# Last two pairs of f tiles in another order on TensorE, last stores in other pieces, and a new order of all work

## The chip, the cores and the metric

The kernel runs on one core of one Trainium2 chip. The metric is the device time of one execution in microseconds (us). The kernel before has a median of 643.3 us over 3 runs, 641.54 to 643.62 us. The engines are PE (TensorE, matrix products; PEld is its loading of weights), DVE (VectorE), ACT (ScalarE), POOL (GpSimd) and SP (SyncE, which here only issues transfers). "SPq" and "ACTq" in rows are the sequencers that issue a transfer (DMA).

## The reference

There are 8 batches with 8 heads, 576 tokens and head size 64. Each batch first attends from 32 packed queries `p` to all keys and values, then from all tokens to those 32 packed results; the outcome goes through a feed-forward network with an ELU.

```
p_packed = softmax(p k^T / sqrt(64)) v          # per batch and head: 32 x 64
x        = softmax(q p_packed^T / sqrt(64)) p_packed
x        = x as 4608 tokens x 512
h        = x @ w_in                              # 512 -> 2048
g        = where(h > 0, h, exp(min(h, 0)) - 1)
out      = g @ w_out                             # 2048 -> 512
```

All inputs and outputs are float32.

## The kernel before, in words

**Stages.** Per batch, the packed attention (scores at L637, exponentials L654, transposition L783, product with `v` L815, transposition of the packed result L851, `ppT`), then the scores of the tokens against the 32 packed results (L876) and their softmax on DVE and ACT (L887 to L929). The product x @ w_in is folded: the packed result times `w_in` is made once per batch (L998, `m_hi`/`m_lo`), and the hidden layer is a product of the attention weights `a` with it. The hidden layer has 16 tiles of 128 rows ("f tiles"). Precision comes from splitting each float32 operand into a high and a low part in a rounded format, so that three products stand for one.

**Stretches.** The tokens of a batch are worked in two windows of 256 and 320 tokens. 512 of the 576 tokens go through the windows; the 64 left over of each batch are stored in DRAM (`rest_dram`) as hidden rows, and those of four batches together are worked off as one more stretch of 256 tokens beside the windows of the last batch. In the first two batches each f tile is a product with `w_out` of its own (L1543, then L1658 to L1661). From batch 2 on, two f tiles are worked as a pair by a scheme with seven products of halves in place of eight (`strassen_pair`).

**One pair.** L1271 makes the hidden rows in PSUM (12 matmuls). ACT and DVE make the ELU (L1283, L1286, L1278) in a buffer `w8`; for the left-over stretch the rows are loaded from `rest_dram` into a buffer `kvq` instead (L1290). Three sums of blocks follow (L1353, on DVE or POOL), then the split into high and low part: a cast on ACT (L428) and a subtraction on DVE (L1361), both into a buffer `g`, of which there are three. The product, L1426, has four groups, one for each of four accumulators in PSUM: 6, 6, 6 and 3 matmuls. The third factor of the groups comes from `swa` (three buffers) and `swb` (two), which SP loads from DRAM for every pair (L1386), and from `wo_a`/`wo_b`, which stay in SBUF.

**The end of a stretch.** After its last pair, a copy on ACT and five additions on DVE (L1458: `add1` and `add2`, `add3`, `add4`, `add5`) make two rows of 128 x 512 outputs out of the four accumulators. `add1` needs the first, `add2` and `add3` the second, `add4` the third and `add5` the fourth. The left-over stretch (in `kvq`) and the last batch's window (in `part`) have their own first three accumulators; the fourth is one PSUM bank for both, so `add5` of the left-over stretch waits until the window's last product in it is done (`run["rest5"]`, L1496). Stores are at L1500: two rows of 256 KB for the left-over stretch, and for the window three pieces: half a row (128 KB), a row on ACT's queue (256 KB), half a row (128 KB).

**The order.** Nothing is scheduled at run time. A table, `ORDER`, lists all 3327 operations in the sequence in which they are written out; the letter behind a number is the engine, where there is a choice. Each engine works its instructions in that sequence and waits on semaphores. `PLACES` gives the PSUM banks. `ONES` says after which operations how many filler matmuls on a tile of ones are issued (L435, `warm_up`), which keep PE busy in the start, where it has no data yet. Operations marked `two` make POOL wait for DVE's last such instruction.

Of the kernel before, what the change touches and what calls it, by code (L numbers as in the profile page):

```python
# [25 lines left out]
0 2 1 7 8 9 10 11 403 404V 405 406V 14 12 416 417V 17 15A 16A 3 4 20 18A 19A 21 13 23A 22A 24 25A  # L26
418 408 5 26 409V 410 400 401A 27 28 29 6 37 48 424 30 425A 402 411 31 32 33 34 529 530A 747 38 39
407G 55 35A 426 412A 413 754 531 748 755 749 40 49 50 56 532A 750 756 751A 414V 757 415G 752G 57 761
41 59 42 758A 759G 43 36 44 419 420A 58 421 753 62 762 763 432 60 65 422V 760 433A 63A 64A 764 768
440 441A 434 442 533 765A 766V 51 61 66A 67V 45 423G 769 534 535 52 770 771 68 69A 435 436A 772V  # L30
773V 775 782 70A 71 437 776 783 767 438V 777 778 72A 551 784 793 427 428A 552 456 439V 785 779A 780G
457A 786A 53 429 430A 431G 557 553 73 794 795 558 458 801 74 75 554 443 444A 787V 796 76 445 802 803
774 797 448 449A 781 450 798V 799G 451 559 77 804 446A 555 447G 806 807A 808G 78 556 810 811 812 813
814 560 561 46A 818 819 820 79 459 788 800 562 80 821 47 54 95 102 789A 805 81 815A 816G 823 84 791A
85 822 452A 453 536 537 824A 827 828 460A 825G 86 87 454A 835 836 837 461 829 455G 840 831 809 830
491 96 817 826 838 538 88 89 832A 833G 82A 83 462A 841A 844 845 90 842V 91 92 504 846 97 852 848 847
463G 505A 499 506 834 843 103 93A 853 94 865 854 492A 849V 850G 855 857 104 858A 106 872 851 866 867
# [12 lines left out]
1013 573 1011 1038A 1045A 115 117A 656G 657G 574 116V 1039V 1046V 658V 540 665V 666G 1031 1048 1049  # L50
1055 1027 1040 1056 1057 1058 1050 655 100 101 142 1051 1032 1062 1069 1052A 663V 664G 659A 660V
1059V 1005 1028 1053V 1063 1060G 1064 1047 1054 1070 1065 661V 662V 667 1066A 1067G 1061 1071 1072
1076 1083 1073A 1074G 1068 1029 1077 1084 1030 669V 1078 541 548 1085 670G 1086 654 1079 549 671V
1080V 1087A 542 543 550 1033 544 1081G 676A 678A 679G 681 677V 672V 118 119A 1088V 1075 673G 1096
1097 1104 120 143 1098 1100 674A 1099 675G 1090 131 1101A 1102G 1113 1082 1105 668 1114 1106 1115
121 122 123 124 125 1109 1089 1103 1110A 144 682G 1107 1116 1117 683V 1118A 1108 1119V 1111V 1121
1122 1123 1124 1130 1126 1127A 684V 689V 1128V 691V 1112 1120 1131 1132 1133 1134 685A 686V 1138
1091 687A 1125 1139 1140 1143 1141 1129 1135A 1136V 1144V 1093 1094 1095 1145G 1147 1155 126 690G
1148 1137 1146 1149 1156 1151 1157 1160 1150 1158 1092 1152A 1153V 127 128 1170 132 133 1161A 1159
1142 688G 1162G 692G 1171 1172 1173 1178 1179 1180 1181 680 1174 1175A 1154 1163 1183 1167 1184A  # L60
1187 1195 695V 1176V 1188 1189 1164 1177 134 1185V 1191 1190 1196 1186 1192A 696G 1182 1168 1169
1193G 1165 1166 1224 697V 698V 135 704V 1197 1200 1194 705G 707 1198 1199 1201A 1204 1212 1202V 1203
1205 1206 699V 700V 701V 1208 1207 1213 1214 1217 1215 1209A 1210V 1218A 1219G 1227 1234 1211 136
137 1228 1229 1230 1241 1235 1236 1237 1220 149 1231A 1232V 1233 138 139 1238A 694 1239G 1242 1243
1244 1225 1248 1245A 1246V 693 702V 703V 708V 709V 1249 706 1250 1251 1255 1256 710V 1257 1258 1252A
1253G 1221 1222 1223 1240 1247 715A 716V 1259A 1260V 717A 711A 712V 713A 714V 719 1262 1269 718V
1283 575 578 1263 1264 1265 721V 722G 720 1270 1271 1226 1272 576 577 1266A 1267V 1276 723V 129A
730A 1254 1261 130 731V 733 728A 729V 724A 725V 726A 727V 581 732 1273A 1274V 734V 579 1289 1286
1268 1275 1277 1278 1279 735G 580 736V 140A 1280A 1281V 737V 1298 738G 1313 582 583 1290 1304 743A
744V 739A 740V 1291 741A 742G 150 152 1292 746 153 154 745 156 157 1305 151 1282 1319 155 1287 584  # L70
1306 1307 1293G 1294G 1284 1295G 1296 1297 1334 1320 141 158 1308V 1309V 1310G 1321 1322 1323V 1324V
1325V 1311 1312 1299 159 162 1326 1327 1335 1336 1337 1338G 145 1339G 1328 1300 1301 1302 1303 1340G
160 1314 164 1349 1315 1316 1343 1350 1317 1318 1351 1352 1353G 1354G 585 1330 1331 586 1355V 1332
1341 1342 1356 1364 1288 1365 1357 1366 1329 1333 1367 1368V 1369V 1370G 1379 1380 1381 1382 1383V
1345 163 1346 1344 1347 1348 1360 1358 1361 165 146 1384V 1385V 1371 1372 1386 1387 1394 1395 166
167 1416 1396 161 1417 1418 1397 1420 1398G 1419 1362 1399V 168 169A 1359 1363 1375 1400V 1421 1373
1388 1401 170V 171 172A 1216 1402 1422 1423 1424 1426 1438 1439 1440 1441 1427G 1428V 1376 1377 1443
1374 1378 1442 1444 1445 1448 1446 147 148 173 1429G 1430 1449G 1450G 174 175 176 1285 1425 1431
# [116 lines left out]
    "623476764764674507501234454664670460126723064647676765045614653204545465456450456120457365777777"  # L195
    "7777032105674333330"
)
ONES = {0: 3, 8: 8, 17: 4, 21: 3, 24: 2, 26: 16, 529: 7}


@with_exitstack
def packed_attention_elu_ffn(
# [22 lines left out]
    nc = tc.nc  # L225
# [3 lines left out]
    NF = w_in.shape[0]  # L229
# [1586 lines left out]
```

## Time and profile before

| | |
|---|---|
| median of 3 runs | 643.3 us (641.54 to 643.62) |
| the profiled execution's own time | 642.62 us |
| its span, first to last instruction | 640.8 us |
| PE, PEld, DVE, ACT, POOL busy | 98%, 88%, 83%, 65%, 26% |
| granted PE clock over the span | 0.998 |
| moved by DMA | 160.43 MB, 250 GB/s on the mean |

In the timeline a row has the start in us from the span's first instruction, the duration in us, the engine, the source line, the operation, the output tile, `<-` and the input tiles, the sizes, and `xN` where N instructions are merged into one row. In square brackets stands how long the engine had been idle before and what ended the wait. A matmul's row is longer than its slot, because matmuls overlap: the distance between the starts of two rows tells the rate, not the length.

### The profile page before, as it was taken

The numbers are of one execution on the slowest core, as the hardware profiler recorded it, in microseconds if no ns is written. First come the engines' busy times: TensorE is split into PE (matmuls) and PEld (weight loads), VectorE is DVE, ScalarE is ACT, GpSimd is POOL, SyncE is SP. The second block draws the span as 40 slices with busy tenths as digits, with TensorE's granted clock in tenths as the row PEclk, the third lists the DMA queues.
The fourth block names the chain that finished last, engine by engine and source line by source line (L and its number), as shares of the span: only waits on it lengthen the run. The fifth ranks groups of instructions, "written<-read, shape, count | busy, mean of one in ns | idle before, by whom it ended". The sixth has DMA issues, their size and how long they took to land.

```text
span 640.8 us, 16120 instructions
## 1 busy us (share of the span) xinstructions
PE 630.3 (98%) x6130; PEld 561.9 (88%) x6130; DVE 534.7 (83%) x1093; ACT 418.9 (65%) x796; POOL 164.9 (26%) x258
## 2 busy tenths in 40 slices
PE   9999999999999999999999999999999999999996
PEld 4567988889789888999989897999889998999996
DVE  3999988779999789878886998898788989667756
ACT  3789987566677657755776577656566667545452
POOL 1224223433232311222123232123111322113121
PEclk9999999999999999999999999999999999999999
DMA  9985795656489978887888989888877777565762
GB/s 346 374 279 197 246 320 166 230 158 225 143 296 307 277 240 280 286 299 231 297 277 276 269 264 317 271 296 301 252 267 272 224 217 245 170 201 189 230 195 82
DMA packets 85405, 160.43 MB, mean 250 GB/s; under 512 B 24272, under 2 KB 40144, under 8 KB 85200
## 3 DMA queue, kind: packets, MB, share of 16 engines
q1 hardware_dynamic: 85040, 158.88, 75.3%
q8 instruction: 48, 0.79, 0.5%
q10 hardware_dynamic: 288, 0.52, 0.2%
q14 instruction: 29, 0.24, 0.1%
HBM read 132.90 MB, written 26.48 MB: 249 GB/s over the span
## 4 chain that ended last, share of the span: by engine, by line
PE 85%; DVE 5%; DMA 5%; ACT 1%; issue 1%; POOL 1%; SPq 0%; DVEq 0%; POOLq 0%; ACTq 0%
PE psum L1426 37%; PE psum L1271 20%; PE psum L1543 6%; PE psum L998 4%; PE psum L1658 4%; PE psum L1661 4%; PE psum L1659 4%; PE psum L435 2%; PE psum L815 2%; DMA kvq<-in_qT 2%; DMA swb<-swb_dram 2%; PE psum L876 1%; DMA out<-part 1%; PE psum L1536 1%; DVE part L1458 1%
## 5 line engine op out<-in xcount | busy, mean ns | idle before, releaser
L1353 POOL TENSOR_TENSOR w<-w 128x128 f32<-128x128 f32 (+1 forms) x167 | 93.8, 565 | 298.5 <-DVE w L1278 77.7
L428 ACT CAST g<-w 128x896 fp32r<-128x896 f32 x96 | 90.0, 940 | 61.2 <-POOL w L1353 28.7
L1361 DVE TENSOR_TENSOR g<-w,g 128x896 fp32r<-128x896 f32 x96 | 104.6, 1092 | 16.6 <-ACT g L428 15.6
L1271 PE MATMUL psum<-a_hi,m_hi 128*128 128x256 f32 (+1 forms) x384 | 112.5, 293 | 0.0
L1271 PE MATMUL psum<-a_lo,m_hi 128*128 128x256 f32 (+1 forms) x384 | 110.2, 287 | 0.0
L1271 PE MATMUL psum<-a_hi,m_lo 128*128 128x256 f32 (+1 forms) x384 | 110.2, 287 | 0.0
L1426 PE MATMUL psum<-wo_b,g 128*128 128x256 f32 x672 | 94.2, 276 | 0.0
L1426 PE MATMUL psum<-wo_a,g 128*128 128x256 f32 x672 | 93.8, 276 | 0.0
L1426 PE MATMUL psum<-swa,g 128*128 128x256 f32 x672 | 93.5, 275 | 0.2 <-DMA swa<-swa_dram 0.2
L1426 PEld LDWEIGHTS psum<-wo_b,g 128*128 128x128 f32 x672 | 84.3, 192 | 4.8 <-issue 4.0
L1426 PEld LDWEIGHTS psum<-wo_a,g 128*128 128x128 f32 x672 | 84.3, 192 | 3.1 <-issue 1.3
L1426 PEld LDWEIGHTS psum<-swa,g 128*128 128x128 f32 x672 | 84.4, 192 | 0.4 <-DMA swa<-swa_dram 0.4
L1271 PEld LDWEIGHTS psum<-a_hi,m_hi 128*128 128x128 f32 x384 | 73.2, 191 | 9.5 <-issue 2.8
L1271 PEld LDWEIGHTS psum<-a_lo,m_hi 128*128 128x128 f32 x384 | 73.3, 191 | 0.1
L1271 PEld LDWEIGHTS psum<-a_hi,m_lo 128*128 128x128 f32 x384 | 73.2, 190 | 0.0
L1283 ACT ACTIVATE e<-psum 128x320 f32<-128x320 f32 x96 | 41.2, 431 | 31.9 <-PE psum L1271 31.3
L1426 PE MATMUL psum<-swb,g 128*128 128x256 f32 x336 | 56.5, 277 | 0.8 <-DMA swb<-swb_dram 0.6
L1426 PEld LDWEIGHTS psum<-swb,g 128*128 128x128 f32 x336 | 46.6, 192 | 3.4 <-issue 2.2
L1278 DVE SCALAR_TENSOR_TENSOR w<-e,psum 128x256 f32<-128x256 f32 x96 | 39.1, 414 | 9.8 <-ACT e L1286 8.4
L1286 ACT ACTIVATE e<-e 128x320 f32<-128x320 f32 x96 | 44.4, 470 | 2.5
L1353 DVE TENSOR_TENSOR w<-w 128x128 f32<-128x128 f32 (+1 forms) x121 | 40.8, 342 | 6.0 <-POOL w L1353 3.8
L1278 DVE SCALAR_TENSOR_TENSOR w<-w,psum 128x512 f32<-128x512 f32 x48 | 32.7, 683 | 13.7 <-ACT w L1286 12.2
(143 smaller groups left out, 1222.5 us busy)
## 6 DMA issues: line engine op xcount, KB each, us to landing
swa<-swa_dram SPq DMA_DIRECT2D x96, 512.0 KB, 5.0
swb<-swb_dram SPq DMA_DIRECT2D x96, 256.0 KB, 4.0
kvq<-in_v SPq DMA_DIRECT2D x16, 640.0 KB, 6.2
raw<-in_w_out SPq DMA_DIRECT2D x16, 511.8 KB, 5.5
raw<-in_w_in SPq DMA_DIRECT2D x16, 511.8 KB, 6.1
kvq<-in_kT SPq DMA_DIRECT2D x14, 576.0 KB, 6.2
kvq<-in_qT SPq DMA_DIRECT2D x14, 576.0 KB, 5.7
out<-part SPq DMA_DIRECT2D x28, 256.0 KB, 4.5
```

The costliest lines, as they stand in the source:

```text
L428: (nc.scalar.copy if e == "ACT" else nc.vector.tensor_copy)(out=out, in_=in_)
L998: nc.tensor.matmul(ps.t[cols_of(pair), g, :w], lhsT=st.ppT.t[rows_of(g), pair, :], rhs=w_in_sb[rows_of(g), pair, c * FC + part * w:c * FC ...
L1271: nc.tensor.matmul(ps, lhsT=m_b[p].t[:, g, o:o + P], rhs=in_turn(st.a.t[q][:, g, cols]), start=(n == 0), stop=(n == 3 * G - 1),)
L1278: nc.vector.scalar_tensor_tensor(out=out, in0=e_, scalar=-1.0, in1=ps, op0=ALU.add, op1=ALU.max)
L1283: nc.scalar.activation(out=out, in_=ps, func=AF.Relu, scale=-1.0)
L1286: nc.scalar.activation(out=x, in_=x, func=AF.Exp, scale=-1.0)
L1353: eng(e).tensor_tensor(out=out, in0=x, in1=y, op=o)
L1361: nc.vector.tensor_tensor(out=g_b.all[:, 7 * P:(7 + b1 - b0) * P], in0=blocks(b0, b1), in1=g_b.all[:, :(b1 - b0) * P].bitcast(F32), op=ALU ...
L1426: nc.tensor.matmul(a.t[:, at * H:(at + rhs.shape[1]) * H], lhsT=operand(blk, p), rhs=rhs, start=new and n == k == 0, stop=a.final == (u, m ...
L1543: nc.tensor.matmul(ps_b.t[:, :n_tok], lhsT=m_b[x].t[:, g, o:o + P], rhs=in_turn(st.a.t[y][:, g, cols]), start=(n == 0), stop=(n == 3 * G - 1),
L1658: nc.tensor.matmul(a.t, lhsT=g_b.t[0][:, t], rhs=w[0], start=first, stop=False)
L1659: nc.tensor.matmul(a.t, lhsT=g_b.t[0][:, t], rhs=w[1], start=False, stop=False)
```

## The change

Four parts. (1) In the last two pairs of the last batch, the pairs are written out together: both pairs of the left-over stretch first, then both pairs of the last window; and the window's groups are chained by accumulator: the fourth accumulator of both pairs, then the first, the second and the third. (2) At the end of a stretch that is the second window of the last batch, `add5` comes before `add4`, the first row is stored in one piece after `add5`, and the second row in two halves after `add4`, one on SP's queue and one on ACT's. (3) `ORDER`, `PLACES` and `ONES` are new throughout. (4) An option that was off (`MIX`) is gone, and the buffers that a pair shares are kept per pair (`shared[u]`).

```diff
-0 2 1 7 8 9 10 11 403 404V 405 406V 14 12 416 417V 17 15A 16A 3 4 20 18A 19A 21 13 23A 22A 24 25A
...
+0 2 1 7 8 9 10 11 ... (all of the table is new)
-ONES = {0: 3, 8: 8, 17: 4, 21: 3, 24: 2, 26: 16, 529: 7}
+ONES = {0: 3, 8: 10, 17: 2, 21: 8, 24: 2, 529: 8, 37: 11}
...
-    MIX = 0
+    N_TAIL = 2
...
             a.last = run["out"]
-            if both and MIX:
-
-                a.last.after = [run["pair"].pop(0)]
-                for x in run["pair"][:1]:
-                    x.after = [a.last]
-            else:
-                run["pair"].append(a.last)
+            if both and win and u >= NF // 2 - N_TAIL:
+                tail.append(a.last)
...
+            late = both and win
+            if late:
+                y = op(q, {"DVE": 0.42}, add5, [y, acc[3].last], use=[part, acc[3]])
+                y5 = y
             y = op(q, {"DVE": 0.69}, add4, [y, acc[2].last], use=[part, acc[2]])
             y4 = y
-            y = op(q, {"DVE": 0.42}, add5, [y, acc[3].last], use=[part, acc[3]])
+            if not late:
+                y = op(q, {"DVE": 0.42}, add5, [y, acc[3].last], use=[part, acc[3]])
...
-            if both:
+            if late:
+                op(q, {"DMA": 0.7}, lambda e: store(e, (0,)), [y5], use=[part])
+                op(q, {"DMA": 0.5}, lambda e: store(e, (1,), slice(0, H)), [y], use=[part])
+                op(q, {"ACT": 0.1}, lambda e: store(e, (1,), slice(H, E), nc.scalar), [y], use=[part], lag=2.7)
+            elif both:
                 op(q, {"DMA": 0.5}, lambda e: store(e, (0,), slice(H, E)), [y3], use=[part])
...
             if f % 2 == 0:
+                late = b == B - 1 and win and f >= NF - 2 * N_TAIL
                 if b == B - 1:
                     strassen_pair(i, B + win, 0, f)
-                strassen_pair(i, b, win, f)
+                if late and f < NF - 2:
+                    continue
+                for n in reversed(range(N_TAIL if late else 1)):
+                    strassen_pair(i - 2 * n, b, win, f - 2 * n)
...
+    before = tail[0].after
+    for x in [tail[n + 4 * m] for n in (3, 0, 1, 2) for m in range(N_TAIL)]:
+        x.after, before = before, [x]
```

**PE's last matmuls before.** Four pairs of 21 matmuls follow each other: left-over and window of the last pair but one (`g_8911`, `g_8929`), then left-over and window of the last pair (`g_8938`, `g_8978`). Of the four, the rows of the last three:

```order
L1426 MATMUL psum_102<-wo_b_969,g_8929 128x256 x6
L1426 MATMUL psum_102<-swa_8780,g_8929 128x256 x6
L1426 MATMUL psum_102<-wo_b_969,g_8929 128x256 x6
L1426 MATMUL psum_102<-swb_8946,g_8929 128x256 x3
L1426 MATMUL psum_102<-wo_b_969,g_8938 128x256 x6
L1426 MATMUL psum_102<-swa_8973,g_8938 128x256 x6
L1426 MATMUL psum_102<-wo_b_969,g_8938 128x256 x6
L1426 MATMUL psum_102<-swb_8976,g_8938 128x256 x3
L1426 MATMUL psum_102<-wo_b_969,g_8978 128x256 x6
L1426 MATMUL psum_102<-swa_8973,g_8978 128x256 x6
L1426 MATMUL psum_102<-wo_b_969,g_8978 128x256 x6
L1426 MATMUL psum_102<-swb_8976,g_8978 128x256 x3
```

PE's last matmuls now; `g_8943` is the left-over stretch's last pair (its last but one, `g_8861`, stands just ahead), `g_8946` and `g_8960` are the window's last two pairs:

```order
L1424 MATMUL psum_102<-wo_b_1015,g_8943 128x256 x6
L1424 MATMUL psum_102<-swa_8963,g_8943 128x256 x6
L1424 MATMUL psum_102<-wo_b_1015,g_8943 128x256 x6
L1424 MATMUL psum_102<-swb_8975,g_8943 128x256 x3
L1424 MATMUL psum_102<-swb_8917,g_8946 128x256 x3
L1424 MATMUL psum_102<-swb_8975,g_8960 128x256 x3
L1424 MATMUL psum_102<-wo_b_1015,g_8946 128x256 x6
L1424 MATMUL psum_102<-wo_b_1015,g_8960 128x256 x6
L1424 MATMUL psum_102<-swa_8922,g_8946 128x256 x6
L1424 MATMUL psum_102<-swa_8963,g_8960 128x256 x6
L1424 MATMUL psum_102<-wo_b_1015,g_8946 128x256 x6
L1424 MATMUL psum_102<-wo_b_1015,g_8960 128x256 x6
```

The number of matmuls is the same. The fourth accumulator (the rows with `swb`) is done 36 matmuls before the end, and the window's last `g` is needed 18 matmuls earlier than before.

**DVE's last additions before** (`kvq` is the left-over stretch, `part` the window; 128x2x256 is `add2`, 128x512 is `add4`):

```order
L1458 TENSOR_TENSOR kvq_8987<-kvq_8987,psum_102 128x512
L1458 TENSOR_TENSOR part_85<-part_85,psum_102 128x256
L1458 TENSOR_TENSOR part_85<-part_85,psum_102 128x2x256
L1458 TENSOR_TENSOR part_85<-part_85,psum_102 128x256
L1458 TENSOR_TENSOR kvq_8987<-kvq_8987,psum_102 128x256
L1458 TENSOR_TENSOR part_85<-part_85,psum_102 128x512
L1458 TENSOR_TENSOR part_85<-part_85,psum_102 128x256
```

DVE's last additions now:

```order
L1451 TENSOR_TENSOR kvq_8971<-kvq_8971,psum_102 128x512
L1451 TENSOR_TENSOR kvq_8971<-kvq_8971,psum_102 128x256
L1451 TENSOR_TENSOR part_85<-part_85,psum_102 128x256
L1451 TENSOR_TENSOR part_85<-part_85,psum_102 128x2x256
L1451 TENSOR_TENSOR part_85<-part_85,psum_102 128x256 x2
L1451 TENSOR_TENSOR part_85<-part_85,psum_102 128x512
```

The left-over stretch is finished before the window begins, and the window's `add4` is the last instruction.

**ACT in the start before**, from its first exponentials (L654) on; `tops` is the first of two steps that turn a loaded weight tile (`raw`) into words, `ppT` the packed result of batch 0:

```order
L654 ACTIVATE tmp,sm<-psum,mx 128x576 x2
L428 COPY tmp<-psum 128x512
L428 COPY tmp<-psum 64x128
L428 COPY tmp<-psum 128x512
L428 COPY tmp<-psum 64x128
L837 ACTIVATE pp<-psum,ri 128x64 x2
L428 COPY ppT<-psum 128x128
```

ACT in the start now:

```order
L428 CAST tops<-raw 128x512 x2
L654 ACTIVATE tmp,sm<-psum,mx 128x576 x2
L428 COPY tmp<-psum 128x512
L428 COPY tmp<-psum 64x128
L428 COPY tmp<-psum 128x512
L428 COPY tmp<-psum 64x128
L428 COPY ppT<-psum 128x128
```

Two casts of weights, of the first tile of `w_out` and of `w_in`, which DVE did before, stand ahead of the exponentials, and the scaling L837 has gone to DVE. On SP the third tile of `w_in` is loaded ahead of the first part of `q`, and not behind it. On PE, by `ONES`, 8 fillers stand between L815 and L851 and not 3; between the first and the second L876 stand the first L998 and 8 fillers, and not 16 fillers; and the first two f tiles' hidden products (L1536, now L1542) are followed by two more, and not by one, before the first product with `w_out`. In batch 1's exponentials, two `tops` casts and a cast of `g` stand between the two L654 on ACT, where before there were an L1561 and an L1567.

## Rows read from the trace of the kernel before

**Rows 1.** The profile's page: the span, and PE's share of it.

```profile
span 640.8 us, 16120 instructions
PE 630.3 (98%) x6130; PEld 561.9 (88%) x6130; DVE 534.7 (83%) x1093; ACT 418.9 (65%) x796; POOL 164.9 (26%) x258
```

**Rows 2.** PE's waits: line, what ended it, us in total, times, longest.

```profile
PE psum L1658 <- ACT tmp L654: 1.5, 1, 1.5
...
PE psum L876 <- DMA kvq<-in_qT: 0.8, 2, 0.5
PE psum L1426 <- DMA swb<-swb_dram: 0.6, 1, 0.6
```

**Rows 3.** Timeline of the start, all engines.

```profile
9.02 0.74 ACT L654 ACTIVATE tmp<-psum,mx 128x576 f32<-128x576 f32 x1 [6.81 <-DVE mx L648]
...
12.19 1.73 PE L815 MATMUL psum<-kvq,tmp 128*32 128x64 f32 x80
...
14.58 0.33 PE L851 MATMUL psum<-ident,pp 128*128 128x128 f32 x1
...
15.27 0.66 PE L876 MATMUL psum<-q,ppT 64*32 64x256 f32 x16
15.87 3.63 PE L435 MATMUL psum<-part 128*128 128x512 bf16 x16
...
16.20 0.77 ACT L428 CAST tops<-raw 128x512 f16<-128x512 bf16 x1 [0.98 <-DMA raw<-in_w_in]
...
20.91 0.71 DVE L929 STREAM_TRANSPOSE k<-tmp 128x512 f32<-128x512 f32 x1
...
22.08 1.89 PE L1536 MATMUL psum<-k,m_hi 128*128 128x256 f32 x8
```

**Rows 4.** Timeline of PE alone, two products of batch 1's attention.

```profile
33.59 1.50 PE L815 MATMUL psum<-kvq,tmp 128*32 128x64 f32 x80
...
40.81 0.72 PE L876 MATMUL psum<-kvq,ppT 64*32 64x288 f32 x16 [0.21 <-DMA kvq<-in_qT]
```

**Rows 5.** Loads of `w_in` issued at 2.10 and 5.97: KB, us to landing.

```profile
raw<-in_w_in SPq DMA_DIRECT2D x1, 511.8 KB, 6.9
...
raw<-in_w_in SPq DMA_DIRECT2D x1, 511.8 KB, 10.1
```

**Rows 6.** The chain that ended last, pieces near 380: start, us, what.

```profile
380.55 1.63 SPq L1225
382.23 4.28 DMA swa<-swa_dram
```

**Rows 7.** Timeline of the end, all engines.

```profile
625.87 0.95 ACT L428 CAST g<-kvq 128x896 fp32r<-128x896 f32 x1 [0.26 <-PE psum L1426]
...
627.39 1.62 DVE L1361 TENSOR_TENSOR g<-kvq,g 128x896 fp32r<-128x896 f32 x1
...
630.62 1.09 DVE L1361 TENSOR_TENSOR g<-w,g 128x896 fp32r<-128x896 f32 x1 [1.61 <-ACT g L428]
...
631.63 2.27 DVE L1458 TENSOR_TENSOR kvq<-kvq,psum 128x256 f32<-128x256 f32 x4
...
632.70 0.83 PE L1426 MATMUL psum<-wo_b,g 128*128 128x256 f32 x6
...
633.98 1.65 DVE L1458 TENSOR_TENSOR part<-part,psum 128x256 f32<-128x256 f32 x3
...
634.71 0.50 PE L1426 MATMUL psum<-swb,g 128*128 128x256 f32 x3
635.55 0.41 DVE L1458 TENSOR_TENSOR kvq<-kvq,psum 128x256 f32<-128x256 f32 x1
...
635.88 1.01 DVE L1458 TENSOR_TENSOR part<-part,psum 128x512 f32<-128x512 f32 x2
```

**Rows 8.** Stores to `out` issued at 635.66 and at 637.05: KB, us to landing.

```profile
out<-part SPq DMA_DIRECT2D x1, 128.0 KB, 1.8
...
out<-part SPq DMA_DIRECT2D x1, 128.0 KB, 2.8
```

More of the change, by code (lines that the diff above doesn't have):

```diff
@@ new lines @@
+1447 173 1463 1466 1467 1468 1469 1390 1391 1392 1464 1393 1405 174 1470 1471G 1433 175 176 1452
+1482 1453 1487 1483 1484 1485 1486 1488 1406 1472G 1409A 1410 1473V 1489 1490 1492 1493G 1411 1412
+1407 1408 1413 1494G 1495V 1414 1474 1475 177 1432 1454 1476 1504 1509 178 1505 1506 1510 1511 1434
+1435 1436 1437 1456 1457 1458 1508 196 1514 179 1496 1507 1512 1526 1527 1531 184 180 181 1455 1477
+1459 1497 1515V 1516V 1491 1528 1529 1530 1415 1478 1532 1533 1534 1536 1548 185 1553 1517G 1518
+1479 1480 182A 186 187 1513 1481 183 1519 1537V 1538G 1549 188 1498 1550 1552 189 1500 1501 1554
@@ new lines @@
+1594 1646 1647 1590 1591 1595 1617 1616 1665 1649 1650 1651 213 1652 1653 1596 209 1638 596 1597 212
+215 1636 1666 1667 1668 1659 1654V 1618 1670 1655G 1656G 216 1681 217 1671 1672 1669 218 1619 1620
+1675 1673 1639 1676V 1677V 1678G 1674 1687 1692 597 1640 1657 1641 1658 1688 1693 1689 1690 1642
+1691 1661 1694 1695 1660 1679 1697 1709 1714 1710 1698G 1699G 598 1680 1696 1700G 1711 1712 1713
+1715 1716 1719 219 220 1662 1663 1664 1717 1701 1702 1731 1736 1732 1733 1737 1738 1720V 1721G 1722V
@@ new lines @@
+1913V 1925 1882 1926 1927 1897 1914G 1915V 1928V 1929V 1930V 1918 255 259 256 257 1885 1886 1898
+1899 1900 260 263 1902A 245V 1903 250 251 1901 1904 1916 1931 1905 1906 1907 1917 258 1932 246 1939
+1919 261 1954 264 262 267 604 1940 1955 1941 1942 1956 1920 1921 1922 1957 1923 1935 1934 1943V
+1944V 265 269 1945G 1933 1936 605 1937 1938 1946 606 1958G 1969 1959V 1960G 1984 1947 607 268 608
+1949 1948 1950 1951 1952 1961 1970 1962 1953 1971 1965 1985 1972 1973V 1974V 270 1975V 1999 1986
+1987 1988V 1963 1966 1989V 1990G 1976 1991 1977 1992 1964 2000 2001 2002 2003V 271 2004G 1967 1968
@@ new lines @@
+2177 2197 2200 2198 2143 307 308 312 298A 299 2179G 310 315 309 2201G 311 2144 2145 2164 2180V 313
+2184 316 2181V 2182 2183 2219 2220 2221 2222 2224 2225 2202V 2203V 2165 2166 2226 2223 2204 2227
+2163 2167 2186 2229 2230G 2205 314 317 320 2231G 2241 2242 2185 2246 2232G 2247 2243 2206 612 2187
+2188 2189 2245 2199 2248 2235 2244 2208 2209 2210 2249 318 322 2251 2252G 2253G 2254G 613 303 304
+2207 614 2228 2212A 2233 2250 2213 2263 2268 2264 2265 2269 2214 2215 2216 2270 2234 319 2211 2217
+2266 2271 615 618 2267 2273 616 617 2237 2255 2256 619 323 2285 2286 2287 2289 2290 2274G 2275G
@@ L1128, in strassen @@
         return S_FIRST <= (b, win)
-    held_ready, last_plain = {}, {}
+    held_ready, last_plain, shared, tail = {}, {}, {}, []
     def strassen_weights(u):
@@ L1378, in strassen_pair @@
         if both:
-            sw, ld = run["shared"]
+            sw, ld = shared[u]
         else:
@@ L1382, in strassen_pair @@
             sw = {0: a_b, 1: a_b, 3: b_b}
-            run["shared"] = sw, ld
+            shared[u] = sw, ld
             for ring, y, dram, n in (("swa", a_b, swa_dram[u].rearrange("p n e -> p (n e)"), 0), ("swb", b_b, swb_dram[u], 3)):
@@ L1417, in strassen_pair @@
         last = u == NF // 2 - 1
-        if not both:
-            run["pair"] = []
         for a, group in zip(acc, groups):
```

314 lines of the change are left out of this document (146 added, 168 removed).

## The prediction

> **What bounds the kernel now.** I read the page first, then PE's waits, then the timeline of the start and of the end. PE is busy for 630.3 of 640.8 us [rows 1]: whatever does not shorten PE's work or its waits, or the stretch behind its last matmul, changes nothing. Between the start and the end PE hardly waits: apart from one wait of 1.5 us in the start, the two largest kinds sum to 0.8 and 0.6 us, both for loads [rows 2]. The start is a chain: PE has no data and works off fillers (L435), while the packed attention of batch 0 goes from engine to engine [rows 3]. The end is a chain too. PE's slot is 0.112 us: from 632.70 to 634.71 it issues 18 matmuls [rows 7]. So its last three end at 634.71 + 0.33 = 635.04; I call this E. DVE's ten additions run without a break from 631.63 = E - 3.4 to 635.88 + 1.01 = 636.89 = E + 1.85 [rows 7]. The last store is issued at 637.05 and takes 2.8 us to land [rows 8], at E + 4.8; the span ends at E + 5.8, 1.0 us behind it. The profiled execution took 642.62 us, 1.8 more than its span; it lies 0.7 below the median of 643.3 and inside its runs. The sum is made against 642.62.
>
> **The end, part by part.** The number of matmuls is unchanged, so E moves only where PE waits or the start moves.
>
> *The last `g`.* The window's last `g` is now wanted 39 slots (4.36 us) before E, and not 21 slots (2.35 us). It can be cast only when the buffer of three pairs ago is free, which is when the left-over stretch's last but one pair is done, 63 slots or 7.04 us before E. A cast takes 0.95 and a subtraction 1.09 [rows 7]; with some 0.35 for three handovers, which is my estimate, `g` is there 2.4 us later, at E - 4.65. That leaves 0.3 us, so no wait: cost 0, and at most 0.5 if the subtraction takes the 1.62 us that one of its kind took [rows 7]. The hidden rows behind it are no later: PE makes them 1.7 us earlier against E than before (15 matmuls more stand behind them).
>
> That 1.62 us subtraction ran beside an addition on POOL. The Trainium skill, in "SBUF — State Buffer", section "Who interferes with whom", says that a DVE instruction with two inputs in SBUF contends with a GpSimd instruction that reads SBUF. The row agrees, and the rule speaks against an order that leaves 0.3 us; by it the sum would be some 0.2 us higher. I leave it out, because POOL's last addition feeds this very `g`, and so is over when the subtraction starts.
>
> *The additions.* DVE begins them when the last subtraction is over, at E - 4.65. The left-over stretch's five take 2.27 + 0.41 = 2.7 us and end at E - 1.95; they no longer wait for PE's last matmul, since the shared fourth accumulator is done at E - 4.0. The window's `add1` follows; `add2` needs the second accumulator, 12 slots before E, so it starts near E - 1.1. `add2` and `add3` are about 1.2 of the 1.65 us that three took, so they end near E + 0.1; `add5` (0.41) ends at E + 0.5 and `add4` (the rest of the 1.01 us, 0.7) at E + 1.15. Before, the last addition ended at E + 1.85: 0.7 us are gained.
>
> *The stores.* Before, 0.9 MB of stores were issued from 635.66 to 637.05. The first, alone, took 1.8 us for 128 KB; the last, behind the others, 2.8 [rows 8]. Now the left-over stretch's 512 KB leave at about E - 1.8 and land beside PE's work; the first row follows at E + 0.65, and the two halves are issued at E + 1.3 with only that row ahead. The trace does not show this mix. It is bounded by 1.8 and 2.8; I take 2.05, nearer to the empty queue, since 256 KB and not 0.9 MB are in flight. They land at E + 3.35, and the span ends at E + 4.35 and not E + 5.8: the end gains 1.5 us, between 0.7 (2.8 us) and 1.7 (1.8 us).
>
> That a half goes through ACT's queue I count as nothing but its time of issue. A store behind others takes longer here, whichever queue they came from [rows 8]. The Trainium skill says the same in "DMA: Bandwidth & Descriptors", section "Issuing engines are not separate DMA queues": all run on the same 16 engines, and a second issuing engine saves only the sequencer's time. Were the queues separate, the end would gain 1.7 us and not 1.5.
>
> **The start.** Here the new order costs.
>
> *Two casts ahead of the exponentials.* ACT now casts two weight tiles before L654. The second lands at 2.10 + 6.9 = 9.0 [rows 5]; the cast takes 0.77 [rows 3], so L654 begins at 9.8 and not 9.02. L815 is two halves, the first of which needs the first exponential alone. So it need not lose the whole 0.75: I take 0.25.
>
> *Fillers.* Behind L815 stand 8 fillers and not 3. Sixteen take 3.63 us, so the five more cost 1.1, and L851 goes from 14.58 to 15.9. L876 follows 0.7 later as before, at 16.6 and not 15.27. `q` is not what it waits for: the first part of `q` takes the place of the load that landed at 5.97 + 10.1 = 16.1 [rows 5]. From L876 a chain of DVE and ACT runs to the end of L929, 20.91 + 0.71 - 15.27 = 6.35 us [rows 3]. It ends at 22.95, when the first hidden product (22.08 before, held up by fillers) can begin: 0.9 us later. The fillers between the two L876 and behind them (8 and 11) end before that.
>
> *The wait of 1.5 us.* [rows 2] PE's first product with `w_out` waited for `g`. Now two more hidden products, about 1 us, stand there, and `g` is made earlier, because POOL no longer has a weight tile ahead of it. So this wait goes. What is late next is the second half of the transposition L783 of batch 1: on ACT, two `tops` casts of 0.77 and a cast of `g` now stand ahead of the second L654, and PE waits some 1.4 us there. L815 of batch 1, at 33.59 before [rows 4], comes out at 34.4. It frees the buffers into which the next `q` is loaded, for which L876 at 40.81 already waited 0.21. The start therefore costs 0.8 us. Both ends: 0.7 us gained, if the second wait does not come (1.5 less 0.8), and 1.9 lost, if none of the fillers' 1.1 us is taken up and L815's first half is as late as L654.
>
> **The middle.** All the rest is laid out anew too. The work, the buffers and the loads are the same; PE has its next matmul ready nearly always, and neither order shows a closer turn of `g`, `swa` or `swb` buffers there than the other. I cost it at 0, between 1.4 gained (both kinds of waits for loads gone) and 2.0 lost.
>
> **Sum.** 640.8 + 0.8 + 0 - 1.5 = 640.1 us of span; with the 1.8 outside, 641.9 us, 0.1% under the profiled execution.
>
> **Rivals.**
> *The start is free.* L783's second half finds its data, so that the 1.5 us wait is really gone, and one of the load waits goes too: 642.62 - 1.5 - 0.7 - 0.3 = 640.1 us. For it: the chain from 22 to 33 us has other work of PE at hand, and the first `g` is earlier. Against it: ACT's order, with three casts ahead of the second L654.
> *Slower: loads held up on SP.* SP issues in order. At 380.55 a store of left-over rows held it for 1.63 us, and the load of `swa` behind it took 4.28 more [rows 6]. The new sequence of loads and stores is another one throughout. Where a load is issued less than those 4.3 us before its first matmul, PE pays the difference. Two such places at 1.6 us each, the time of that wait, give 641.9 + 3.2 = 645.1 us. For it: PE's waits in the middle are all for loads [rows 2]. Against it: they sum to 1.4 us over some 600.
> *The end gains nothing to speak of.* The halves still land 2.8 us after their issue and a late `g` holds PE for 0.5: 0.7 - 0.5 = 0.2 us gained, 643.2 us. For it: the bound of 2.8 is a row. Against it: most of those bytes leave earlier now.
>
> **Chances.** The forecast has 0.48, the free start 0.28, the held-up loads 0.18, the empty end 0.06. About 0.3% (1.9 us) is what a measurement of this kernel can tell from no change. Below 640.7 lies nearly the free start alone, with the forecast's lower edge: faster 0.30. Above 644.5 lie the held-up loads and a start at its worst: slower 0.19. Between: 0.51. The range runs from 640.0, the free start, to 645.0, nearly the held-up loads; the likeliest case alone has 640.9 to 643.4. I put 641.9.
>
> **What would show it.** In the new trace: L654 at 9.8; L876 near 16.6; the first hidden product near 23.0; a wait of PE in the middle of L783 near 31; L815 of batch 1 near 34.4. At the end: no wait of PE in its last 84 matmuls; the left-over stretch's stores issued before PE's last matmul; the last addition 1.15 us and the end of the span 4.35 us behind E. In between, PE's waits for loads of about 1.4 us in all. I am wrong if these waits pass 3 us, if batch 1's L815 comes at 33.6 or earlier, or if the end of the span is 5 us or more behind E.

## The result, and the profile after

The changed kernel takes 647.57 us (median of 8 runs, 645.99 to 650.77), the kernel before 642.71 (8 runs, 641.54 to 643.62). The ratio is 1.0083, with a 95% interval of 1.0061 to 1.0104: slower by 4.9 us, where 641.9 was forecast. The profiled execution, at 645.99 us, is the fastest of the eight. Its page, against [rows 1]:

```profile
span 644.2 us, 16123 instructions
...
PE 631.6 (98%) x6128; PEld 562.2 (87%) x6131; DVE 529.5 (82%) x1088; ACT 419.5 (65%) x799; POOL 164.5 (26%) x260
```

The span is 3.4 us longer. PE's waits, against [rows 2] (line, what ended the wait, us in total, times, longest):

```profile
PE psum L1424 <- DVE w L1278: 1.6, 1, 1.6
PE psum L1424 <- DMA swb<-swb_dram: 1.2, 2, 0.7
...
PE psum L1424 <- DMA swa<-swa_dram: 0.7, 2, 0.5
PE psum L815 <- DMA tmp<-turn_dram: 0.7, 1, 0.7
...
PE psum L876 <- DMA kvq<-in_qT: 0.4, 1, 0.4
```

The wait of 1.5 us in the start is gone. A single wait of 1.6 us for DVE, in the product L1424, has come, and the loads sum to 3.0 us (1.6 before).

**The start.** All engines, against [rows 3], and the two last rows against [rows 4]:

```profile
9.79 0.73 ACT L654 ACTIVATE tmp<-psum,mx 128x576 f32<-128x576 f32 x1
...
16.55 0.66 PE L876 MATMUL psum<-q,ppT 64*32 64x256 f32 x16
...
23.05 1.32 PE L1542 MATMUL psum<-k,m_hi 128*128 128x256 f32 x5 [0.39 <-DVE k L929]
...
30.36 1.55 PE L783 MATMUL psum<-ident,tmp 128*128 128x128 f32 x10
...
33.73 1.70 PE L815 MATMUL psum<-kvq,tmp 128*32 128x64 f32 x80
...
40.97 0.72 PE L876 MATMUL psum<-kvq,ppT 64*32 64x288 f32 x16
```

The second product L876 of batch 1 stood at 40.81 before: at 41 us the changed kernel is 0.16 us behind. That is one execution: in all 16 traces with the changed start this product begins at 40.5 to 42.8, 41.3 on the mean, and in the four with the old start at 40.5 to 41.8, 40.9 on the mean.

**The end.** All engines, against [rows 7]:

```profile
632.98 0.94 ACT L428 CAST g<-w 128x896 fp32r<-128x896 f32 x1 [1.39 <-PE psum L1424]
...
633.95 1.09 DVE L1361 TENSOR_TENSOR g<-w,g 128x896 fp32r<-128x896 f32 x1 [1.11 <-ACT g L428]
...
637.58 0.82 SPq L1498 DMA_DIRECT2D out<-kvq  x2
...
638.47 1.50 PE L1424 MATMUL psum<-wo_b,g 128*128 128x256 f32 x12
638.67 2.20 DVE L1451 TENSOR_TENSOR part<-part,psum 128x512 f32<-128x512 f32 x4 [0.52 <-PE psum L1424]
```

Twelve slots of 0.112 from 638.47 give E = 639.81. The additions end at 640.87 = E + 1.06 and the span at E + 4.4; before it was E + 5.8. The two halves took, against [rows 8]:

```profile
out<-part ACTq DMA_DIRECT2D x1, 128.0 KB, 2.2
out<-part SPq DMA_DIRECT2D x1, 128.0 KB, 1.9
```

The end gains 1.4 us. But E itself has moved from 635.04 to 639.81, by 4.8: with 0.16 of it in the start, 4.6 us were lost in the middle. The largest piece is one place. All engines there (rows of weight loads and most hidden products left out):

```profile
593.72 0.68 DVE L1451 TENSOR_TENSOR part<-part,psum 128x512 f32<-128x512 f32 x1
594.17 0.60 ACT L1283 ACTIVATE w<-psum 128x512 f32<-128x512 f32 x1 [1.69 <-PE psum L1271]
...
594.78 2.47 ACTq L1498 DMA_DIRECT2D out<-part  x1
...
596.31 0.83 PE L1424 MATMUL psum<-swa,g 128*128 128x256 f32 x6
597.29 0.63 ACT L1286 ACTIVATE w<-w 128x512 f32<-128x512 f32 x1 [2.53 <-issue]
...
597.95 0.69 DVE L1278 SCALAR_TENSOR_TENSOR w<-w,psum 128x512 f32<-128x512 f32 x1 [2.22 <-ACT w L1286]
...
598.70 0.94 PE L1424 MATMUL psum<-wo_a,g 128*128 128x256 f32 x6 [1.55 <-DVE w L1278]
...
599.84 0.38 PE L1271 MATMUL psum<-a_hi,m_hi 128*128 128x256 f32 x1 [0.21 <-DVE w L1278]
```

Read from the top: `add4` of the last batch's first window ends at 594.40, and ACT issues the row that it completes as a store. The issue takes 2.47 us. Behind it waits the exponential L1286, behind that the ELU on DVE, and behind that PE: the third accumulator of the second window is given, by `PLACES`, the PSUM bank that these hidden rows lie in. The next hidden product waits again for the next ELU, its weight load for 0.4. Together some 2 us. The other 2.6 us are more waits for loads (3.0 against 1.6) and small pieces.

In the kernel before the same store stood ten instructions further on in ACT's order, behind casts, and its issue took 0.37:

```profile
599.74 0.94 ACT L428 CAST g<-w 128x896 fp32r<-128x896 f32 x1
602.82 0.95 ACT L428 CAST g<-kvq 128x896 fp32r<-128x896 f32 x1 [2.14 <-issue]
602.84 0.37 ACTq L1500 DMA_DIRECT2D out<-part  x1
```

### The profile page after: what moved, and what is told of

Its sections match the earlier page's. It is cut to its first block, busy times and chain, and to the rows that moved or that the text cites. A ratio compares the mean times of both kernels' runs of the same rounds, so it can differ in the third digit from the quotient of the medians.

```text
span 644.2 us, 16123 instructions
## 1 busy us (share of the span) xinstructions
PE 631.6 (98%) x6128; PEld 562.2 (87%) x6131; DVE 529.5 (82%) x1088; ACT 419.5 (65%) x799; POOL 164.5 (26%) x260
## 4 chain that ended last, share of the span: by engine, by line
PE 81%; DMA 6%; ACT 4%; DVE 4%; issue 1%; SPq 1%; ACTq 0%; POOL 0%; DVEq 0%; POOLq 0%
PE psum L1424 37%; PE psum L1271 18%; PE psum L1549 5%; PE psum L998 4%; PE psum L1664 3%; PE psum L1665 3%; PE psum L1667 3%; DMA swa<-swa_dram 2%; DMA swb<-swb_dram 2%; PE psum L815 2%; PE psum L876 1%; DMA raw<-in_w_in 1%; DMA tmp<-turn_dram 1%; PE psum L1542 1%; ACT tops L428 1%
## 5 line engine op out<-in xcount | busy, mean ns | idle before, releaser
L1353 POOL TENSOR_TENSOR w<-w 128x128 f32<-128x128 f32 (+1 forms) x160 | 92.3, 579 | 286.7 <-DVE w L1353 101.0
L1424 PE MATMUL psum<-wo_a,g 128*128 128x256 f32 x672 | 94.0, 276 | 1.6 <-DVE w L1278 1.6
L1424 PE MATMUL psum<-swa,g 128*128 128x256 f32 x672 | 93.8, 276 | 0.7 <-DMA swa<-swa_dram 0.7
L1424 PE MATMUL psum<-wo_b,g 128*128 128x256 f32 x672 | 93.7, 276 | 0.0
L1424 PEld LDWEIGHTS psum<-wo_a,g 128*128 128x128 f32 x672 | 84.3, 192 | 5.0 <-issue 2.1
L1424 PEld LDWEIGHTS psum<-wo_b,g 128*128 128x128 f32 x672 | 84.0, 192 | 4.0 <-issue 4.0
L1424 PEld LDWEIGHTS psum<-swa,g 128*128 128x128 f32 x672 | 84.2, 192 | 3.4 <-DMA swa<-swa_dram 1.1
L1283 ACT ACTIVATE e<-psum 128x320 f32<-128x320 f32 x96 | 41.2, 430 | 41.5 <-PE psum L1271 37.2
L1424 PE MATMUL psum<-swb,g 128*128 128x256 f32 x336 | 56.7, 279 | 1.2 <-DMA swb<-swb_dram 1.2
L1424 PEld LDWEIGHTS psum<-swb,g 128*128 128x128 f32 x336 | 46.5, 192 | 5.6 <-DMA swb<-swb_dram 3.8
L1353 DVE TENSOR_TENSOR w<-w 128x128 f32<-128x128 f32 (+1 forms) x128 | 43.1, 340 | 8.5 <-POOL w L1353 6.3
L1286 ACT ACTIVATE e<-e 128x320 f32<-128x320 f32 x96 | 44.6, 470 | 2.6
```

The costliest lines, as they stand in the source:

```text
L1283: nc.scalar.activation(out=out, in_=ps, func=AF.Relu, scale=-1.0)
L1286: nc.scalar.activation(out=x, in_=x, func=AF.Exp, scale=-1.0)
L1353: eng(e).tensor_tensor(out=out, in0=x, in1=y, op=o)
L1424: nc.tensor.matmul(a.t[:, at * H:(at + rhs.shape[1]) * H], lhsT=operand(blk, p), rhs=rhs, start=new and n == k == 0, stop=a.final == (u, m ...
```

## The experiments

Theory M says that the order of the middle costs the time, the issue on ACT above all. Its rivals are the granted clock, the changed end, and loads held up on SP. In the diffs 3149 is L1283, 3150 is L1286, and 3109 is the store. Ratios are to the kernel before, run on the same chip in the same turns (five rounds), with 95% intervals.

**e1_again**: nothing altered.

> The changed kernel once more, with nothing altered. Theory M (the new order of the middle costs it): PE's waits between 41 and 600 us recur at the same places and sum to about 6 us, against some 2.4 in the kernel before; the largest, 1.6 and 0.4 us near 597 to 600, stands again behind the store issue on ACT's queue (2.47 us). Rival J (that one execution was odd): the issue takes 0.4 us as in the kernel before, and the waits stand elsewhere. Rival C (the granted clock): several executions of the changed kernel have a mean granted clock of 0.996 to 0.998, and not 1.000; a profile of such a one shows a stretch at half clock, worth some 1 to 2 us, and PE's waits are as before.

648.33 us, 1.0066 [1.0045, 1.0086]. The issue is long again, 2.87 us, and PE waits 1.9 and 0.3. The waits for loads stand partly elsewhere and sum to 2.0.

**e2_store_later**

```diff
-... 3149 3107 3109 3150 ... 3181 3188V 3223 ...
+... 3149 3107 3150 ... 3180 3109 3181 3188V 3223 ...
```

> The changed kernel, in which one operation is moved: the store on ACT's queue at the end of the last batch's first window stands behind four more activations and two more casts, about where the kernel before has it, and not between L1283 and L1286 of a pair's hidden rows. Theory M: ACT no longer stands still there, the waits of 1.6 and 0.4 us near 597 to 600 go, and the time falls by 2.0 us against the changed kernel, from 647.6 to 645.6 (ratio to the kernel before 1.005). Rival (the wait there is one for DVE, or for the closer turn of the pair's hidden rows and its product): the wait stays, at 1 us or more, and the time at 647.6.

643.90 us, 0.999 [0.997, 1.0011]: 4.4 us less than e1, from one moved operation. ACT's timeline:

```profile
593.67 0.60 ACT L1283 ACTIVATE w<-psum 128x512 f32<-128x512 f32 x1 [1.69 <-PE psum L1271]
594.30 0.63 ACT L1286 ACTIVATE w<-w 128x512 f32<-128x512 f32 x1
...
602.18 0.38 ACTq L1498 DMA_DIRECT2D out<-part  x1
```

The issue takes 0.38, and PE waits nowhere between 590 and 610. That is twice what the wait alone would give back, and twice what was expected.

**e3_tail**

```diff
-ORDER, PLACES, ONES of the changed kernel
+ORDER, PLACES of the kernel before for the first 3240 operations, of the changed one for the last 87; ONES of before
```

> The kernel before in its start and middle (its order of operations, its PSUM banks, its fillers) with the changed end alone: last two pairs chained by accumulators, add5 ahead of add4, the stores in the new pieces. Theory M: the end gains 1.4 us and nothing else moves, 642.7 - 1.4 = 641.3 us. Rival T (the changed end makes the window's g or its loads late, and its price hid in the shift of PE's end): 643 us or more, with a wait of PE in the last 84 matmuls.

643.15 us, 0.998 [0.996, 1.0]. From the start of PE's last matmul to the end of the span it is 4.5 us, as in every kernel here with the changed end, and 5.9 in those with the old one: the end gains 1.4 us. This execution also waited 2.1 us for a load of `q`, and what follows shows a second price that a wait can have (columns: stretch, its length, then PE, PEld, DVE, ACT, POOL busy, the granted clock, DMA share, GB/s):

```profile
210.00:214.00 4.00, 2.90 (x24) 2.67 (x22) 2.13 (x8) 2.86 (x7) 0.91 (x2) 1.00 1.00 314
214.00:216.00 2.00, 1.00 (x17) 0.33 (x17) 0.06 (x1) 0.31 (x1) 1.18 (x2) 0.84 1.06 346
216.00:218.00 2.00, 2.00 (x8) 2.00 (x9) 1.92 (x3) 0.10 (x1) 0.00 (x0) 0.50 1.07 374
218.00:220.00 2.00, 2.00 (x15) 2.00 (x14) 1.90 (x5) 1.55 (x4) 0.00 (x0) 0.81 0.55 215
```

Behind the wait the clock falls to 0.50, 1.2 of 2.4 GHz: 8 matmuls in 2 us where 15 fit. That loses 2 x (0.16 + 0.50 + 0.19) = 1.7 us, nearly as much as the wait.

**e7_longer**

```diff
-3150: L1286
+3150: L1283 once more, L1286
```

> The changed kernel with L1283 of that one pair issued a second time behind the store on ACT (the same values once more), which makes ACT, and so PE's wait, some 0.6 us longer. Theory C2 (a long wait of PE is paid twice: while it waits, and by a granted clock that falls behind it): the wait is some 2.2 to 2.6 us, the profile shows 0.5 of the clock for about 3 us behind it, and the time is 0.6 + 1.5 = 2 us above the changed kernel in the executions that had no fall of the clock, so about 649 to 650. Rival (waits cost what they last): 0.6 us above the changed kernel, 648.9, with a clock of 1.00 from 596 to 608.

648.64 us (7 runs), 1.0058 [1.0032, 1.0084]: by the ratio not above e1's 1.0066, where theory C2 asked for 2 us more and its rival for 0.6. The time thus decides nothing. The profiled execution does show what C2 says of a single wait: the issue took 2.66, PE waited 2.4, and the clock fell right behind it:

```profile
596.00:600.00 4.00, 1.63 (x15) 1.44 (x13) 0.91 (x3) 1.96 (x4) 0.00 (x0) 1.00 0.70 238
600.00:604.00 4.00, 3.92 (x19) 3.62 (x20) 2.26 (x4) 1.32 (x2) 1.18 (x2) 0.58 0.02 4
```

4 x 0.42 = 1.7 us. It does not come each time. Of the ten waits of PE of 1.6 us or more past 41 us, in all traces, those of 1.9 (e18), 2.1 (e3) and 2.4 (e7) had a fall behind them; the other seven, of 1.6 to 2.1, had none, the one of 2.1 in e9 among them, at the same product as e3's.

In the traces with the changed end a fall in the middle goes with a mean clock of 0.996 over the span, and those without have 0.998 or more. Of the 20 executions of the changed kernel (the first eight and e1) 11 have a mean of 0.997 or less, of the 72 of e2, e5, e6, e10, e15 and e18, whose issue is short, four. So a wait of some 2 us and, in every second execution, a fall of 1.7 make about 3 of the 4.4 us. The rest stays open, and falls are not all of the spread: the slowest of the eight, 650.77, has a mean of 0.998. That the fall followed the wait is seen in e3, e7 and e18; that it does so in an ordinary run of the changed kernel is inferred from the means.

**e5_store_sp**, **e6_store_behind_exp**, **e10_next_pair**: the store at the same place on SP; one place later; three places later.

```diff
-op(q, {"ACT": 0.1}, lambda e: store(e, (1,), on=nc.scalar), [y4], ...)
+op(q, {"DMA": 0.5}, lambda e: store(e, (1,)), [y4], ...)          # e5
-... 3107 3109 3150 3151 ... 3134 3174 3175 ...
+... 3107 3150 3109 3151 ... 3134 3174 3175 ...                    # e6
+... 3107 3150 3151 ... 3134 3174 3109 3175 ...                    # e10
```

> The changed kernel with the same store of 256 KB at the same place in the order, but issued by SP and not by ACT. Theory M (what costs is that ACT, which has the next exponential behind it, is held while it issues): ACT is free, the wait of PE near 597 to 600 is gone, and the time is that of the kernel with the store moved, about 4.4 us below the changed kernel (near 643.9, ratio to the kernel before 0.999), whether or not SP now shows a long issue. Rival (the store's transfer itself disturbs the loads at that place): a wait of PE of 1 us or more stays between 594 and 602, and the time is above 645.5.

> The changed kernel with the store one place later on ACT: behind the exponential of the pair's hidden rows (L1286) and ahead of the next pair's L1283. If the long issue belongs to that moment (some 595 us), ACT is again held 2 to 3 us, but the pair whose product is wanted next has its exponential done: PE's wait of 1.6 us shrinks to under 0.5 us for that pair, and a smaller one may come for the next hidden rows; 644 to 646 us. If the long issue hangs on the instruction ahead of it and not on the moment, the issue takes 0.4 us, no wait is left, and the time is near 643.9. Rival (the order of DVE is at fault): 648 as the changed kernel.

> The changed kernel with the store three places later on ACT, between L1283 and L1286 of the next pair. Between these two the issue was long three times (2.5 to 2.9 us), one place behind L1286 it took 0.37. If a place between these two instructions makes the issue long, it is 2 us or more here too, and PE waits up to 2 us for the next pair (645 to 648 us). If it was the moment (the store's data had been added up only 0.4 us before), the issue takes 0.4 us and the time is near 644.

644.00, 644.24 and 644.19 us; 1.0011 [0.9986, 1.0035], 1.0013 [0.9991, 1.0034], 1.0004 [0.9985, 1.0024]. The issues took 0.34, 0.37 and 0.38 us, and nothing waits there. e6 falls on the same moment, behind `add4`, and e10 on the same place, between the two activations: neither alone makes the issue long.

**e9_before_moved**, **e11_ahead**: the kernel before with its store between L1283 and L1286; the changed kernel with it one place earlier.

```diff
+... 3149 ... 3106 3109 3150 ...       # e9, in the order of the kernel before
-... 3149 3107 3109 3150 ...
+... 3107 3109 3149 3150 ...           # e11
```

> The kernel before with one operation moved: its store on ACT's queue, which stood ten instructions further on, now stands between L1283 and L1286 of the hidden rows that are wanted next, as in the changed kernel. Theory M (the place alone makes the cost): ACT is held some 2.5 us in the issue, PE waits 1 to 2.5 us between 593 and 602, and the time is 1 to 4 us above the kernel before. Rival (it takes the changed order around it): the issue takes 0.4 us and the time is that of the kernel before within 1 us.

> The changed kernel with the store one place earlier on ACT, ahead of L1283 and behind a cast. It has to wait for add4 (at 594.4) and is issued at the same moment as in the changed kernel, but not behind L1283. If the moment makes the issue long: 2 to 3 us again, L1283 and L1286 late by as much, 648 us or more. If the place behind L1283 does: an issue of 0.4 us, ACT late by under 1 us, PE's wait under 0.5 us, near 644.5.

e9: 643.90 us, 1.0004 [0.9989, 1.0018], an issue of 0.38: theory M as it stood, that the place makes the cost, falls. e11: 646.43 us, 1.0037 [1.0018, 1.0055]; the issue took 0.38, but L1283 came late because the store, ahead of it, waited for `add4`. By the starts of its matmuls PE lost only some 0.7 us there; what the rest of e11's 2 us above the versions with a short issue is stays open.

**e13_relu_first**, **e14_add4_early**: is it the wait for the data? One execution each, not timed in rounds.

```diff
-3149: L1283
+3149: L1283 twice                     # e13
-... 3130 3131 3106 3140 ...
+... 3130 3106 3131 3140 ...           # e14
```

> The changed kernel with L1283 of that one pair issued twice ahead of the store (the same values once more), so that add4 is done, and nothing is waited for, when ACT comes to the store. Theory W (the issue is long where it has to wait for its data behind an activation that is still running): 0.4 us, and no wait of PE over 0.5 us near 600. Rival P (it is long at this place, whatever it waits for): 2 us or more, and PE waits 2 us or more.

> The changed kernel with add4 of that stretch done one DVE instruction earlier, ahead of the subtraction of a g, so that the store's data is there some 1 us before ACT comes to it. Theory W (the issue is long where it has to wait for its data): 0.4 us, no wait of PE over 0.5 us near 600. Rival P (long at this place, whatever it waits for): 2 us or more, and PE waits 1.5 us or more.

e13 has an issue of 0.37. e14 has the data 1.1 us before the issue, and it took 2.93: theory W falls. But the four long issues have something in common. Rows of the queue that the page calls `instruction`, in the changed kernel from 595.7 to 596.2 (queue, kind: packets, MB, share):

```profile
q14 instruction: 1, 0.01, 5.2%
```

An 8-KB transfer of instructions begins at 595.74, inside the issue, and lands at 596.15; the issue ends 1.1 us later. In e1, e7 and e14 it lies inside as well, and the issue ends 1.2 us behind its landing each time. The issues of e1 and e14:

```profile
595.12 2.87 ACTq L1498 DMA_DIRECT2D out<-part  x1
```

```profile
596.19 2.93 ACTq L1498 DMA_DIRECT2D out<-part  x1
```

In e6, e10 and e13 it lies 3.0 to 3.8 us ahead of the issue, in e11 2.4 behind.

**e15_four_more**, **e16_one_more**, **e18_one_more_timed**

```diff
-    nc.scalar.activation(out=warm, in_=ebias, func=AF.Exp, scale=0.0)
+    for _ in range(5):                # 2 in e16 and e18
+        nc.scalar.activation(out=warm, in_=ebias, func=AF.Exp, scale=0.0)
```

> The changed kernel, with the first instruction of ACT (an exponential of one column, at the very start, where ACT waits for data) issued five times and not once; place, moment and neighbours of the store stay as they are. Theory F (the issue is long because the fetch of ACT's next instructions falls into it): the fetch comes four instructions earlier and off the store, the issue takes 0.4 us, PE does not wait near 600, and the time is 4 us below the changed kernel, near 644.2 (ratio 1.000 to 1.002). Rival P (the place and what stands around it make the issue long): 2.5 us again and 648.

> The same with one more instruction and not four. Theory F: the fetch moves by one instruction, to L1283 or to the store's own wait; the issue takes 0.4 us if the fetch now begins before the store is reached, and is shorter than 2.5 us if it begins while it is being reached. Rival P: 2.5 us again.

> The changed kernel with one more tiny instruction on ACT at the start, as e16, now timed. Theory F (the fetch on the store is the whole loss, the rest as forecast): 643 to 644, ratio to the kernel before 0.998 to 1.001, no run above 647. Rival (the new middle costs something besides): ratio 1.002 to 1.004, as e15 had, with load waits of over 4 us in sum past 200.

One instruction of one column, at the start of the program, and the issue is short. e16, the same queue from 590.6 to 591.1, and ACT at the place:

```profile
q14 instruction: 1, 0.01, 4.6%
```

```profile
593.09 0.60 ACT L1284 ACTIVATE w<-psum 128x512 f32<-128x512 f32 x1 [1.69 <-PE psum L1272]
593.41 0.38 ACTq L1499 DMA_DIRECT2D out<-part  x1
593.83 0.63 ACT L1287 ACTIVATE w<-w 128x512 f32<-128x512 f32 x1
```

The transfer has moved to 590.67, ahead of the store. e16's one time is 642.58; e15 has 644.15 us, 1.0028 [1.0006, 1.0049], above the 1.000 to 1.002 expected, and e18 644.58 us, 1.0002 [0.9976, 1.0028]. In e18 a load wait of 1.9 us near 279 was again followed by a clock of 0.50, which the expectation (no run over 647) did not allow for.

**e4_start_tail**, **e8_mix**, **e12_start**, **e17_late_scores**: what is left over.

```diff
+e4, e12, e8: order of the changed kernel to 41, 94, 244 us, of the kernel before from there, changed end
+e17: e3, with one batch's second L876 and three operations behind it after the next two hidden products
```

> The changed kernel's start (its order and fillers to batch 1's second scores, near 41 us) and its end, with the order of the kernel before in between. Theory M: the start costs 0.2 us and the end gains 1.4, so 641.5 us, and 6 us less than the changed kernel. Rival C (the new start lets the granted clock fall in some executions): the median lies at 643 or above, with mean clocks of 0.996 to 0.998 in the runs, while the kernel with the old start and middle has none.

> The changed kernel's order to about 244 us, the order of the kernel before from there on, and the changed end. Theory M: it leaves out the long store issue and the changed order's load waits near 278, 304 and 484 (2.2 us in the profile with the store moved) and takes the ones of the kernel before past 244 instead (near 310, 389 and 450, 1.6 us), but not its waits of 1.7 and 2.3 us near 27 and 213: 642.5 to 643.5 us, ratio to the kernel before about 0.998. Rival (load waits come and go with any order): 644 or more.

> The changed kernel's order and fillers to 94 us, the order of the kernel before from there on, and the changed end: what the start costs by itself, against the kernel before with the changed end alone (643.15, ratio 0.998). Theory S (as forecast, the start costs): 0.2 to 0.8 us above it, ratio 0.9985 to 0.9995. Rival (the start gains, since the wait of 1.5 us near 27 is gone): 0.5 to 1.5 us below it, ratio 0.996 to 0.997.

> The kernel before with the changed end (as e3), and one thing more: the second scores of one batch (L876, and their softmax's first steps on DVE) stand behind the next two hidden products on PE, because in three profiles of the old middle PE waited 0.7, 2.3 and 2.3 us there for the load of q, and once the granted clock fell behind it. Theory: the wait falls to 0.6 us or less and no clock falls there, 642 us, ratio to the kernel before 0.996. Rival (the wait comes back one step later, at the next scores or at a load): 643.2, ratio 0.998.

645.72 (1.0028), 643.79 (1.0002 [0.9976, 1.0028]), 645.91 (1.0037) and 642.28 us (0.9984 [0.9958, 1.001]). e4 and e12 settle nothing: where the orders are joined PE waits 2.0 and 1.2 us. e8 shows no gain, where 0.998 was expected. In e17 the load is no longer waited for at that place (0.4 us for an ELU instead), and waits for `q` near 41 (1.0 us) and for `swa` and `swb` near 387 and 444 remain; no version is shown to beat the kernel before by more than its interval.

## Why the prediction was wrong

- **The end, −1.5: right.** No wait in the last 84 matmuls; the last `g` is ready at 635.04, 0.4 us ahead of its first matmul; the stores took 1.9 and 2.2 us (2.05 taken). It measured −1.4.
- **The start, +0.8: mis-sized.** L654 at 9.8, L876 at 16.6 and the first hidden product at 23.0 came as forecast. The wait of 1.4 us in the middle of batch 1's L783 did not: its ten matmuls ran through from 30.36, and L815 came at 33.73 and not at 34.4. The start cost 0.16 us at 41, and 0.3 on the mean of the traces here.
- **The middle, 0: this step failed.** "The work, the buffers and the loads are the same; PE has its next matmul ready nearly always" looked for closer turns of buffers, and went by totals. It also took PE's waits in the middle to be all for loads; the kernel before has one of 0.4 us for DVE (`PE psum L670 <- DVE m_lo L1011: 0.4, 1, 0.4`), and its loads sum to 1.6 and not 1.4. It did not ask where in ACT's order the store of the first window had moved: from behind a cast to between two activations that DVE and then PE wait for. That was to be seen in the order. That its issue would take 2.5 us and not 0.37 was not: this hangs on where ACT's instructions happen to be fetched. It costs 4 us: six versions with a short issue and otherwise the changed middle (e2, e5, e6, e10, e15, e18) lie at 0.999 to 1.003, the changed kernel at 1.0083 and 1.0066. (e11, with a short issue but ACT held for the data, lies at 1.0037.)
- **Loads held up on SP**: the rival named a time near the truth (645.1) for a wrong reason. Waits for loads between 41 and 638 us sum to 1.2 to 3.9 us in 13 profiles of the changed middle, 2.6 on the mean, and to 1.6, 3.2 and 3.2 in three of the old one (before, e3, e9). The 3 us that I had named as the limit come up with the old middle too.
- What is left: the six versions lie 0.1% above the kernel before on the mean, and not 0.1% below. Four of the six intervals hold the forecast (641.9 to 642.62, 0.9989), two lie just above it. e3, the old start and middle with the changed end, lies at 0.998: the new start and middle thus seem to cost some 1.8 us beside the long issue, but the intervals overlap. One piece can be seen. In five of the 13 profiles of the changed middle (e1, e5, e7, e14, e15) PE stands still for 0.8 to 1.1 us near 415, inside a product L1424 with `wo_a`, and the profile names nothing that it waited for; none of the seven with the old middle there (before, e3, e4, e8, e9, e12, e17) has this. The rest stays open.

## What to carry to other kernels

A store issued by an engine that computes is an instruction in that engine's chain: place it where nothing that is waited for stands right behind it, or give it to SP. When all of an order is new, follow each issue on a computing engine's queue and each PSUM bank that passes from a short-lived tile to an accumulator; totals by engine don't show them. A long wait of PE can cost up to twice its length: the granted clock fell to 0.50 behind waits of 1.9, 2.1 and 2.4 us in three traces, though not behind seven others of 1.6 to 2.1.

## What the runs showed of the hardware

A transfer of instructions that begins while ACT issues a DMA goes with an issue of 2.5 to 2.9 us (four traces) where the other 35 issues on ACT in these runs took 0.34 to 0.40. The queue's row does not name the engine; that the transfer is ACT's follows from e16, where one more instruction of ACT, over a thousand ahead in its stream, moved it off the store. The Trainium skill, "Runtime: NRT & Kernel Launch", section "Instruction fetch mechanics", says that the sequencer fetches its next block by its own DMA queue while it executes, and that crossing a block is mostly hidden. Of the changed kernel's 29 transfers of 8 KB, ACT's and others', one fell into an issue on ACT and was not hidden; here the measurement decides. What in the issue waits for the fetch no run shows.

SP has long issues too, but beside another engine's transfers. The one of [rows 6], 1.63 us at 380.55, overlaps a transfer of the other instruction queue; the kernel before, from 380.2 to 381:

```profile
q8 instruction: 1, 0.02, 11.3%
```

This queue's transfers of 16 KB are PE's, to judge by their number: there are 48 of them, 0.79 MB, one for every 255 of PE's 12,411 instructions on the mean, and SP has 787 in all. In the changed kernel 14 of SP's 15 issues of 1.0 us or more (past 9 us) overlap such a transfer, and 31 of its 458 issues under 0.7 do; in all 20 traces it is 266 of 298 long ones, and most of these end 0.3 to 0.4 us behind its landing. A transfer alongside is not enough: of 268 issues of SP beside an 8-KB transfer alone, 250 took under 0.7 us. Which issue of SP is long thus moves with PE's instructions; what the long ones cost here was not measured.

PE's wait near 415 ends 1.2 to 1.6 us behind the landing of a transfer of PE's queue in all five traces, much as ACT's long issues ended 1.1 to 1.2 us behind theirs. That PE waited for its instructions there was not tested.
